# Row maxima from 64-row products in both halves of TensorE's array, with a copy of K on VectorE, a third landing place for weights and a new planned order

## The chip, the cores and the metric

One core of a Trainium2 chip runs the whole program. The time is device microseconds (us) of one execution; three executions of the kernel before took 927.57 to 933.28 us, with a median of 932.64 us. The engines are TensorE (PE, with its weight loads PEld), VectorE (DVE), ScalarE (ACT), GpSimd (POOL) and SyncE (SP), which issues the DMAs.

## The reference

```python
def _attn_ref(q, k, v):                       # (4, 8, 1152, 64) each
    q_pool = q.reshape(B, H, S // 2, 2, D).mean(axis=3)
    scores = np.matmul(q_pool, k.transpose(0, 1, 3, 2)) / np.sqrt(D)
    scores = scores - np.max(scores, axis=-1, keepdims=True)
    attn = np.exp(scores)
    attn = attn / (np.sum(attn, axis=-1, keepdims=True) + 1e-09)
    return np.matmul(attn, v)

def _moe_ref(x, w_in, w_out, a, b):           # x: (2304, 512), w_in: (512, 2048)
    h = x @ w_in
    P = a[0] + a[1] * h + a[2] * h**2 + a[3] * h**3
    Q = 1.0 + np.abs(b[0]) * np.abs(h) + np.abs(b[1]) * h**2
    return (P / (Q + 1e-6)) @ w_out
```

The attention has 4 batches of 8 heads, 576 pooled query rows and 1152 keys per head, depth 64. Its output, 2304 rows of 512, goes through an MLP with a rational function.

## The kernel before, in words

**Numbers in two parts.** Each float32 operand is scaled and split into an upper and a lower float16 part. For a pair of heads (a *unit*), `pr_hi` and `pr_lo` write the parts of K side by side into `spk`, and a DMA transpose (`pr_tr`, L689) turns them: tile `k` then has the 64 depth rows of the upper part of K in partitions 0 to 63 and those of the lower part in 64 to 127. Tile `q` has the upper part of Q twice, in both halves, in its first 9 blocks; its next 9 blocks hold the lower part of Q in partitions 0 to 63 and zeros below. Tile `kb` is a copy of the upper part of K in partitions 0 to 63, made by a DMA (`pr_kb`, L692), and a row of ones at partition 64.

**One attention tile** (144 of them, 128 query rows of one head, or in every ninth, the *wide* slot 8, 64 rows of each of two heads): `at_fill` (L720) makes scores of 128 rows by 1152 keys in the three PSUM banks `SC`, in three products of 384 columns and depth 128 (in a wide tile six, each for 64 output partitions); `at_max` (L727, DVE) takes the negated row maxima; `at_turn` (L730) turns them into a row, and `at_row` (L734, ACT) writes it into `q` at partition 64 beside the lower part. `at_fill2` makes the transposed scores in `ST`, per 128 keys one product of depth 128 (L743) and one of depth 65 (L744), which adds the lower part of Q and the maximum. `at_exp` (L751, ACT) exponentiates into 32-bit whole numbers `E`, `at_split` (L759, DVE) scales their 16-bit halves, and `at_pv` (L773) multiplies by three parts of V, 54 products per group of one or two tiles, into unused columns of the same banks `SC` and `ST`. So a bank is shared in turn by PE, DVE and ACT.

**The MLP** works on 18 chunks of 128 rows in 4 steps each (72): `mo_h` (L915, 48 products), a rational function on ACT, DVE and POOL (L928 to L977), `mo_o` (L986 to L988, 12 products of 512 columns).

**The weights** come in 32 pieces of 512 KB (L458, tile `raw`) into two landing places; ACT and POOL read a piece (L467, L471), DVE joins the bits (L475) into the float32 tile `wf`, ACT squares it for the scale (L480); the split parts follow when all 16 pieces of a matrix are there (L502, L506). The first MLP step can't start before both matrices are done, since its tiles reuse that memory (`w_close`).

**The order** of every engine's work is written out by a planner, `Plan`. Each operation is added with an engine, a duration in ns (a DMA with issue, transfer and lead), a due time and what it reads and writes. The planner simulates forward and backward passes over these durations and keeps the order of the shortest one; `PRM["stir"]` can name seeds of random changes that are tried on it and kept where the planned end comes earlier. Engines then run their instructions strictly in that order. All DMAs are issued by SP in one queue.

Of the kernel before, what the change touches and what calls it, by code (L numbers as in the profile page):

```python
# [23 lines left out]
SLACK = 16.0  # L24
# [6 lines left out]
    stir=[],  # L31
# [238 lines left out]
def kernel(  # L270
# [175 lines left out]
    def w_open():  # L446
        st["stg_cm"] = tc.tile_pool(name="stg", bufs=1)
        st["stg"] = st["stg_cm"].__enter__()

    def w_load(n, i):  # L450

        t = st["stg"].tile([P, 512, 2], I32, tag="raw", name=f"raw_{n}{i}", bufs=NRAW)
        st["raw", n, i] = t
        if n == "wi":
            src = w_in.bitcast(I32)[i // 4 * P:(i // 4 + 1) * P, (i % 4) * 1024:(i % 4 + 1) * 1024]
        else:
            src = w_out.bitcast(I32)[i * P:(i + 1) * P, :]
        nc.sync.dma_start(out=t.rearrange("p f w -> p (f w)"), in_=src)  # L458
# [4 lines left out]
    def w_win(n, i):  # L463
        if i == 0:
            st["wf", n] = st["stg"].tile([P, 16, 512], F32, tag="wf", name=f"wf_{n}")
        u = st["raw", n, i][:, :, 1].bitcast(F32)
        nc.scalar.activation(out=st["wf", n][:, i, :], in_=u, func=AF.Prelu, scale=2.0 ** -111, alpha=-(2.0 ** 32))  # L467
# [203 lines left out]
    def pr_lo(j, w):  # L671
        d = pairs[j]
        stt = nc.vector.scalar_tensor_tensor
        if w == "v":
            stt(pr_new(j, "v2"), d["vn"], d["ss"][:, 2:3], d["v1"][:, :, 0:D], ALU.mult, ALU.subtract)
        elif w == "q":
            stt(spq[:, KC:2 * KC, 0, :], d["qn"][:, :, 0, :], d["ss"][:, 1:2], spq[:, 0:KC, 0, :], ALU.mult, ALU.subtract)
# [13 lines left out]
    def pr_kb(j):  # L691
        nc.sync.dma_start(out=pr_new(j, "kb")[0:D], in_=pairs[j]["k"][0:D])  # L692
# [32 lines left out]

    def at_max(t):
        nc.vector.tensor_reduce(mts[t % NM][:, D:D + 1], SC[:, :, 0:TH], AX.XY, ALU.max, negate=True)  # L727
# [4 lines left out]
    def at_row(t):  # L732
        j, slot = tiles[t]
        nc.scalar.activation(out=pairs[j]["q"][D:D + 1, KC + slot, :], in_=TURN[D:D + 1], func=AF.Copy)  # L734
# [289 lines left out]
    def prep(j, part):  # L1024
# [8 lines left out]
        if mode == "again":  # L1033
            if hp < 2:
                for i in (0, 1) if part == 0 else (2, 3, 4):
                    add("dma", cost(256 * op_cols(i)), at[6], lambda i=i: pr_again(j, i), r=[("kept", bb, hp, i)], w=[("set", o, i)], seq=["seqag"])
                if part == 0:
                    add("dma", (625, 820, 624), at[7], lambda: pr_kb(j), r=[("set", o, 1)], w=[("set", o, 5)])
            return
        if part == 1:  # L1040
            add("act", 1240, at[14], lambda: pr_hi(j, "v"), r=["vn", ("ss", j)], w=[("set", o, 2)])
            add("dve", 1500, at[15], lambda: pr_lo(j, "v"), r=["vn", ("ss", j), ("set", o, 2)], w=[("set", o, 3)])
            add("dve", 370, at[16], lambda: pr_v3(j), r=[("set", o, 2)], w=[("set", o, 4)])
# [5 lines left out]
        add("dma", (1400, 1640, 449), at[0], lambda: pr_load_q(j), w=["qn"])  # L1049
        add("dma", cost(128 * 4608), at[1], lambda: pr_load_v(j), w=["vn"])  # L1050
        add("pool", 1500, at[6], lambda: pr_pool(j), w=["qn"])
        add("act", 1146, at[6], lambda: pr_stat(j, 0), r=["kn"], w=[("st", j), "spk"])
        add("act", 700, at[6], lambda: pr_stat(j, 1), r=["qn"], w=[("st", j), "spk"])
        add("act", 1146, at[6], lambda: pr_stat(j, 2), r=["vn"], w=[("st", j), "spk"])
# [7 lines left out]
        for i, w in enumerate(("k", "q")):  # L1062
            add("act", 1240, at[8 + 2 * i], lambda w=w: pr_hi(j, w), r=[w + "n", ("ss", j)], w=["sp" + w])
            add("dve", 820 if w == "q" else 1650, at[9 + 2 * i], lambda w=w: pr_lo(j, w), r=[w + "n", ("ss", j)], w=["sp" + w])
            add("dma", T_TR2, at[9 + 2 * i], lambda w=w: pr_tr(j, w), r=["sp" + w], w=[("set", o, 0 if w == "q" else 1)])
            if w == "k":
                add("dma", (625, 820, 624), at[10], lambda: pr_kb(j), r=[("set", o, 1)], w=[("set", o, 5)])

    def attend(t):
# [7 lines left out]
        add("pe", (650, 1100) if wide else (490, 960), s, lambda: at_fill(t), r=[("set", o, 0), ("set", o, 1)], w=["S"], seq=["seqS"], bank=B_S)  # L1077
        add("dve", 1330, s + 0.6, lambda: at_max(t), r=["S"], w=[M], bank=B_S)
        add("pe", (60, 128), s + 2.1, lambda: at_turn(t), r=[M], w=["TURN"], seq=["seqM"], bank=B_TURN)
        add("act", 230, s + 2.3, lambda: at_row(t), r=["TURN", ("set", o, 0)], w=[("row", t)], bank=B_TURN)  # L1080
        add("pe", (1150, 2304) if wide else (1010, 2304), s + 2.7, lambda: at_fill2(t), r=[("row", t), ("set", o, 0), ("set", o, 1), ("set", o, 5)], w=["T"], seq=["seqT"], bank=B_T)
        add("act", 1300, s + 3.9, lambda: at_exp(t), r=["T", ("esc", jp)], w=[E], seq=["seqE"], bank=B_T)
        add("dve", 780, s + 5.3, lambda: at_split(t), w=[E], seq=["seql"])

    def product(g, host):
# [6 lines left out]
        add("act", 370, s + PRM["pvx"], lambda: at_x(g), r=[V], w=[x], seq=["seqx"], bank=B_PV[g % 2])  # L1092

    def weights(n, s0):
        for i in range(16):
            s = s0 + PRM["ws"] * i
            raw, wf = ("raw", i % NRAW), ("wf", i)
            add("dma", cost(128 * 4096), s, lambda i=i: w_load(n, i), w=[raw], seq=["raw"])
            add("act", 630, s + 4, lambda i=i: w_win(n, i), r=[raw], w=[wf], seq=["win"])
            add("pool", 830, s + 4, lambda i=i: w_low(n, i), w=[(*raw, "low")], r=[raw], seq=["low"])  # L1100
            add("dve", 800, s + 4, lambda i=i: w_bits(n, i), r=[raw, (*raw, "low")], w=[wf])
            add("act", 615, s + 6, lambda i=i: w_stat(n, i), r=[wf], w=[("wst", n, i)])
# [5 lines left out]
        for i in range(8):  # L1108
            wf = [("wf", 2 * i), ("wf", 2 * i + 1)]
            add("act", 1141, s + PRM["wl"] * i, lambda i=i: w_hi(n, i), r=wf + [("sw", n)], w=[(n, 0, i)])  # L1110
            add("dve", 1330, s + PRM["wl"] * i, lambda i=i: w_lo(n, i), r=wf + [("sw", n), (n, 0, i)], w=[(n, 1, i)])
# [48 lines left out]
    def chunk(p):  # L1160
# [6 lines left out]
        add("dve", 420, u - 1.6, lambda: ch_rcp(c), r=xs + svs, w=["ri"])  # L1167
        add("pool", 1400, u - 1.5, lambda: ch_norm(c), r=["ri"], w=xs)
        add("pool", 870, u, lambda: ch_hi(c), r=xs + [("cf", batches(c)), "late"], w=["xs"])
        add("dve", 900, u, lambda: ch_lo(c), r=xs, w=["xs"])  # L1170
# [4 lines left out]
    def step(p, f):  # L1175
# [92 lines left out]
```

## Time and profile before

| | before |
|---|---|
| median of three executions | 932.64 us (927.57 to 933.28) |
| profiled execution | 926.45 us, span of its instructions 924.7 us |
| granted TensorE clock, mean | 0.954 |
| PE busy | 809.6 us, 88% |
| DVE busy | 750.5 us, 81% |
| ACT busy | 620.5 us, 67% |
| POOL busy | 445.4 us, 48% |
| bytes moved by DMA | 88.80 MB |

Busy is the time in which at least one instruction of an engine runs. Matmuls overlap: one of 128 columns is listed with about 220 ns, and the next starts 56 ns after it, so the distance from start to start tells what a product costs PE in a stream. PEclk is the granted clock as a share of 2.4 GHz. An "idle" figure of a row is the engine's idle time just before that instruction, with the instruction or transfer that ended it.

### The profile page before, as it was taken

How to read it: one execution, taken by the hardware profiler on the slowest of the kernel's cores; microseconds unless marked ns; L12 is line 12 of the kernel's file. 1: busy time of each engine (PE TensorE's matmuls, PEld its weight loads, DVE VectorE, ACT ScalarE, POOL GpSimd, SP SyncE). 2: the span in 40 equal slices, each digit the busy share in tenths (PEclk: the TensorE clock that was granted, in tenths of full speed). 3: DMA queues.
4: the chain of work that ended last, by engine and by line, in shares of the span. 5: the costliest groups of instructions: out<-in, count | busy, mean ns of one | idle time of the engine just before them, and what ended most of it. 6: DMA issues, size and time to landing. Idle time of an engine off the chain costs nothing.

```text
span 924.7 us, 27851 instructions
## 1 busy us (share of the span) xinstructions
PE 809.6 (88%) x12196; PEld 640.1 (69%) x12196; DVE 750.5 (81%) x1011; ACT 620.5 (67%) x937; POOL 445.4 (48%) x482
## 2 busy tenths in 40 slices
PE   0687587649999999899899999989999998999997
PEld 0475366537878887677678886777777777887773
DVE  5578887787988988769899888779989867977666
ACT  5579988765767767646856786666767746665452
POOL 3212235315755624458655552446855454445664
PEclk9988778958999999979999999989999999999999
DMA  7587376801600706612501234290917300521000
GB/s 217 160 210 199 80 189 214 222 24 44 135 25 1 155 2 154 144 34 48 119 13 26 44 112 91 73 245 14 236 32 155 70 20 14 164 68 25 24 13 23
DMA packets 121338, 88.80 MB, mean 96 GB/s; under 512 B 96768, under 2 KB 98816, under 8 KB 121216
## 3 DMA queue, kind: packets, MB, share of 16 engines
q1 hardware_dynamic: 121216, 87.02, 38.2%
q8 instruction: 95, 1.56, 0.7%
q14 instruction: 27, 0.22, 0.1%
HBM read 49.24 MB, written 8.87 MB: 63 GB/s over the span
## 4 chain that ended last, share of the span: by engine, by line
PE 54%; DVE 17%; ACT 11%; DMA 6%; issue 5%; POOL 4%; SPq 2%; POOLq 0%; DVEq 0%; ACTq 0%
PE ph_h L915 14%; PE st L743 6%; PE st L744 6%; PE sc L773 6%; PE st L773 5%; PE sc L720 5%; PE po L986 4%; PE po L988 4%; PE po L987 4%; ACT E L751 4%; DVE mt L727 3%; DVE E L759 2%; DVE t L941 2%; DVE g L965 2%; DVE t L937 2%
## 5 line engine op out<-in xcount | busy, mean ns | idle before, releaser
L751 ACT ACTIVATE E<-st,esc 128x1152 int32<-128x1152 f32 x144 | 188.6, 1310 | 68.3 <-PE st L730 45.7
L727 DVE TENSOR_REDUCE mt<-sc 128x1 f16<-128x1152 f32 x144 | 194.8, 1353 | 43.9 <-PE sc L720 32.5
L915 PEld LDWEIGHTS <-wi 128*128 128x128 f16 x3456 | 199.6, 99 | 24.2 <-DVE t L941 15.8
L915 PE MATMUL ph_h<-x,wi 128*128 128x128 f16 x3312 | 201.6, 221 | 10.5 <-DVE t L941 8.6
L743 PE MATMUL st<-q,k 128*128 128x128 f16 (+1 forms) x1440 | 179.4, 222 | 17.6 <-ACT q L734 12.2
L744 PE MATMUL st<-q,kb 65*128 65x128 f16 (+1 forms) x1440 | 179.8, 222 | 2.5 <-DMA kb<-k 2.5
L973 POOL TENSOR_TENSOR e<-t,e 128x512 f32<-128x512 f32 x72 | 111.4, 1547 | 141.3 <-DVE e L969 118.7
L744 PEld LDWEIGHTS <-kb 65*128 65x128 f16 x1440 | 137.8, 102 | 27.2 <-issue 21.0
L773 PEld LDWEIGHTS <-E 128*128 128x128 f16 (+1 forms) x4320 | 146.9, 103 | 11.5 <-issue 7.1
L743 PEld LDWEIGHTS <-k 128*128 128x128 f16 x1440 | 137.7, 102 | 17.2 <-issue 12.3
L759 DVE TENSOR_SCALAR E<-E 128x2304 f16<-128x2304 uint16 x144 | 126.8, 883 | 27.4 <-ACT E L751 27.2
L720 PE MATMUL sc<-k,q 128*128 128x384 f16 (+1 forms) x480 | 104.2, 353 | 41.2 <-DVE mt L727 28.6
L946 POOL TENSOR_SCALAR e<-A,b_abs 128x512 f32<-128x512 f32 x72 | 71.2, 989 | 82.5 <-ACT A L928 82.0
L988 PE MATMUL po<-wo,g 128*128 128x512 f16 x288 | 109.1, 379 | 1.6 <-DVE g L977 1.6
L986 PE MATMUL po<-wo,g 128*128 128x512 f16 x288 | 109.2, 379 | 0.0
L987 PE MATMUL po<-wo,g 128*128 128x512 f16 x288 | 109.1, 379 | 0.0
L950 POOL TENSOR_TENSOR e<-e,A 128x512 f32<-128x512 f32 x72 | 97.1, 1348 | 5.5
L720 PEld LDWEIGHTS <-q 128*128 128x128 f16 (+1 forms) x480 | 40.4, 105 | 73.7 <-issue 44.4
L928 ACT ACTIVATE A<-ph_h,cf 128x512 f32<-128x512 f32 x69 | 47.3, 685 | 58.5 <-PE ph_h L915 56.0
L954 ACT ACTIVATE A<-e,q_one 128x512 f32<-128x512 f32 x72 | 51.9, 720 | 48.3 <-POOL e L950 47.6
L977 DVE SCALAR_TENSOR_TENSOR g<-e,cf,A 128x512 f16<-128x512 f32 x72 | 64.9, 901 | 21.4 <-POOL e L973 21.3
L773 PE MATMUL sc<-v,E 128*128 128x65 f16 (+3 forms) x2160 | 77.3, 198 | 0.0
(124 smaller groups left out, 1175.7 us busy)
## 6 DMA issues: line engine op xcount, KB each, us to landing
kn<-in_k_dram SPq DMA_DIRECT2D x16, 576.0 KB, 4.5
vn<-in_v_dram SPq DMA_DIRECT2D x16, 576.0 KB, 5.2
qn<-in_q_dram SPq DMA_DIRECT2D x16, 512.0 KB, 4.9
raw_wi<-in_moe_w_in_dram SPq DMA_DIRECT2D x16, 512.0 KB, 4.8
raw_wo<-in_moe_w_out_dram SPq DMA_DIRECT2D x16, 512.0 KB, 4.5
kb<-k SPq DMA_DIRECT2D x18, 288.0 KB, 5.0
out_dram<-ob SPq DMA_DIRECT2D x16, 256.0 KB, 3.4
keep<-v SPq DMA_DIRECT2D x4, 292.5 KB, 5.7
```

The lines of the kernel that those rows point to most:

```text
L720: nc.tensor.matmul(SC[ps, jj, 0:TH], d["q"][:, slot, ps], d["k"][:, h * KC + 3 * jj:h * KC + 3 * jj + 3, :].rearrange("p c m -> p (c m)"), ...
L727: nc.vector.tensor_reduce(mts[t % NM][:, D:D + 1], SC[:, :, 0:TH], AX.XY, ALU.max, negate=True)
L743: nc.tensor.matmul(o, d["k"][:, h * KC + c, :], d["q"][:, slot, qs], start=True, stop=False)
L744: nc.tensor.matmul(o, d["kb"][0:D + 1, h * KC + c, :], d["q"][0:D + 1, KC + slot, qs], start=False, stop=True)
L751: nc.scalar.activation(out=d["e"].rearrange("p (a c) -> p a c", a=3), in_=ST[:, :, 0:TH], func=AF.Exp, bias=esc[:, 1:2], scale=esc[:, 0:1],)
L759: nc.vector.tensor_scalar(e.bitcast(F16), e.bitcast(U16), 2.0 ** -6, None, ALU.mult)
L773: nc.tensor.matmul(pv[:, 0:w], e[:, c, qs, part], pairs[j][n_v][:, h * KC + c, :], start=(c == 0 and i == 0), stop=(c == KC - 1 and i == 2),)
L915: nc.tensor.matmul(mo[c, f]["p2"][:, i, :], wi[wl][:, kk, fs], x[:, xl * KD + kk, :], start=(n == 0), stop=(n == 3 * KD - 1))
L973: nc.gpsimd.tensor_tensor(w["e2"], w["t"], w["e2"], ALU.subtract)
L986: nc.tensor.matmul(po, g[0][:, e, :], wo[0][:, kk, :], start=(kk == 0), stop=False)
L987: nc.tensor.matmul(po, g[0][:, e, :], wo[1][:, kk, :], start=False, stop=False)
L988: nc.tensor.matmul(po, g[1][:, e, :], wo[0][:, kk, :], start=False, stop=(kk == KF - 1))
```

## The change

The row maxima are taken from the upper parts of Q and K alone: `at_fill` makes products of depth 64 in place of 128, the first and third of a tile with partitions 0 to 63 (`k`), the second with partitions 64 to 127, where a copy of the upper part of K now lies in `kb`. The exponent's bias has more room for that (`SLACK` 24 in place of 16). The lower part of Q therefore moves to partitions 64 to 127, the row of maxima to partition 0, and the second product of `at_fill2` has depth 128 in place of 65. The copy of K is made by DVE in place of a DMA. Weight pieces 2, 5, 8 and 11 of each matrix land in the last sixteenths of `wf` in place of `raw`. In the planner's table most durations are new, loads are counted at 270 in place of 360 bytes per ns, and 25 seeds are tried.

```diff
-SLACK = 16.0
+SLACK = 24.0
...
-    stir=[],
+    stir=[5001, 5004, 5032, 5039, 5073, 5194, 5227, 5228, 5235, 5238, 5243, 5266, 5295, 5296, 5303, 5333, 5337, 5459, 5480, 5488, 5573, 5643, 5745, 5890, 5998],
...
-    T_COPY, T_TR2 = 450, (625, 3050, 625)
+    T_COPY, T_TR2 = 450, (625, 3300, 625)
     def cost(n_bytes):
-        return (T_COPY, n_bytes / 360.0, T_COPY - 1)
+        return (T_COPY, n_bytes / 270.0, T_COPY - 1)
...
         for t in kbs:
-            nc.vector.memset(t[D:D + 1], 1.0)
-        nc.gpsimd.memset(spq[:, KC:2 * KC, 1, :], 0.0)
+            nc.vector.memset(t[0:D], 0.0)
+            nc.vector.memset(t[0:1], 1.0)
+        nc.gpsimd.memset(spq[:, KC:2 * KC, 0, :], 0.0)
...
+        st["wf", "wi"] = st["wf", "wo"] = st["stg"].tile([P, 16, 512], F32, tag="wf", name="wf")
+    IN_WF = (2, 5, 8, 11)
     def w_load(n, i):
-        t = st["stg"].tile([P, 512, 2], I32, tag="raw", name=f"raw_{n}{i}", bufs=NRAW)
+        if i in IN_WF:
+            t = st["wf", n][:, 14:16, :].bitcast(I32).rearrange("p a (f w) -> p (a f) w", w=2)
+        else:
+            t = st["stg"].tile([P, 512, 2], I32, tag="raw", name=f"raw_{n}{i}", bufs=NRAW)
...
     def pr_kb(j):
-        nc.sync.dma_start(out=pr_new(j, "kb")[0:D], in_=pairs[j]["k"][0:D])
+        nc.vector.tensor_copy(pr_new(j, "kb")[D:P], pairs[j]["k"][0:D])
...
         for jj in range(3):
+            half = slice(D, P) if jj == 1 else slice(0, D)
...
-                    SC[ps, jj, 0:TH], d["q"][:, slot, ps],
-                    d["k"][:, h * KC + 3 * jj:h * KC + 3 * jj + 3, :].rearrange("p c m -> p (c m)"),
+                    SC[ps, jj, 0:TH], d["q"][half, slot, ps],
+                    d[("k", "kb", "k")[jj]][half, h * KC + 3 * jj:h * KC + 3 * jj + 3, :].rearrange("p c m -> p (c m)"),
...
-                nc.tensor.matmul(o, d["kb"][0:D + 1, h * KC + c, :], d["q"][0:D + 1, KC + slot, qs], start=False, stop=True)
+                nc.tensor.matmul(o, d["kb"][:, h * KC + c, :], d["q"][:, KC + slot, qs], start=False, stop=True)
...
-                add("dma", (625, 820, 624), at[10], lambda: pr_kb(j), r=[("set", o, 1)], w=[("set", o, 5)])
+                add("dve", 710, at[10], lambda: pr_kb(j), w=[("set", o, 1)])
...
-        add("dve", 780, s + 5.3, lambda: at_split(t), w=[E], seq=["seql"])
+        add("dve", 870, s + 5.3, lambda: at_split(t), w=[E], seq=["seql"])
...
-        add("dve", 800, u + PRM["m_glo"], lambda: mo_glo(c, f), r=[A], w=[G, E2, T])
+        add("dve", 900, u + PRM["m_glo"], lambda: mo_glo(c, f), r=[A], w=[G, E2, T])
```

The copy writes the resource ("set", o, 1), which `at_fill` reads, so a unit's first scores wait for its copy.

## Rows read from the trace of the kernel before

**Rows 1.** The page's span in 40 slices of 23.1 us: busy tenths of PE.
```profile
PE   0687587649999999899899999989999998999997
```

**Rows 2.** Busy time of the engines in four stretches: up to the first MLP step, then two with attention and MLP steps together and, between them, one almost without MLP steps. Columns: stretch, its length, busy us of PE, PEld, DVE, ACT, POOL with the count of instructions, granted clock, DMA share, GB/s.
```profile
25.00:211.00 186.00, 123.74 (x1754) 97.06 (x1752) 144.93 (x202) 145.93 (x236) 52.39 (x72) 0.83 0.61 161
211.00:331.00 120.00, 116.76 (x1906) 97.99 (x1905) 104.62 (x129) 85.44 (x121) 72.06 (x60) 0.98 0.32 67
331.00:402.00 71.00, 67.22 (x1007) 50.16 (x1004) 54.78 (x87) 46.00 (x69) 25.70 (x50) 0.93 0.46 104
402.00:546.00 144.00, 138.67 (x2147) 112.89 (x2146) 128.83 (x159) 99.38 (x146) 87.78 (x75) 1.00 0.26 60
```

**Rows 3.** The chain of waits up to 215 us, some of its longest pieces. Columns: start, length, what.
```profile
24.99 7.89 DMA kb<-k
...
148.47 3.38 DMA raw_wo<-in_moe_w_out_dram
...
171.45 4.54 DMA raw_wo<-in_moe_w_out_dram
...
178.09 3.05 DMA raw_wo<-in_moe_w_out_dram
...
196.57 9.65 DVE wo L506 x8
...
211.42 3.59 PE ph_h L915 x33
```

**Rows 4.** What the DMA queue on SP waited for before it issued loads of weight pieces (us in total, times, longest), and the issues of the second matrix (ns min/median/max, first and last start).
```profile
SPq L458 <- DVE wf_wi L475: 16.9, 7, 9.8
...
SPq L458 <- DVE wf_wo L475: 11.4, 7, 2.3
...
L458 SPq DMA_DIRECT2D raw_wo<-in_moe_w_out_dram x16: 327/335/715, 125.9 to 180.8; - x16
```

**Rows 5.** PE in order of time around the three score products of an ordinary tile. Columns: start, length of the piece, instruction, shapes, count.
```profile
363.55 0.38 PE L988 MATMUL po<-wo,g 128*128 128x512 f16 x1
363.76 0.65 PE L720 MATMUL sc<-k,q 128*128 128x384 f16 x3
364.25 0.22 PE L743 MATMUL st<-q,k 128*128 128x128 f16 x1
```

**Rows 6.** The same around the six score products of a wide tile, each of which fills 64 columns of the array, in pairs.
```profile
708.88 0.38 PE L988 MATMUL po<-wo,g 128*128 128x512 f16 x1
709.19 0.68 PE L720 MATMUL sc<-k,q 128*64 128x384 f16 x6
709.80 0.39 PE L986 MATMUL po<-wo,g 128*128 128x512 f16 x1
```

**Rows 7.** The same where a product of depth 3 and 4 columns stands between products of depth 128.
```profile
345.27 0.65 PE L720 MATMUL sc<-k,q 128*128 128x384 f16 x3
345.85 0.17 PE L358 MATMUL sc<-diag,onesb 3*128 3x4 bf16 x1
345.96 0.23 PE L743 MATMUL st<-q,k 128*128 128x128 f16 x1
```

**Rows 8.** Groups of instructions by form: the score products of ordinary and of wide tiles. Columns: line, engine, operation, tiles, shapes, count, busy us and mean ns, idle before with its releasers.
```profile
L720 PE MATMUL sc<-k,q 128*128 128x384 f16 x384 | 92.6, 354 | 39.5 <-DVE mt L727 27.2 <-DMA q<-spq 11.3 <-DVE top L350 0.9
...
L720 PE MATMUL sc<-k,q 128*64 128x384 f16 x96 | 11.5, 350 | 1.7 <-DVE mt L727 1.5 <-ACT xf L790 0.2
```

**Rows 9.** Waits after 210 us: how long the maxima stood for the score products (us in total, times, longest).
```profile
DVE mt L727 <- PE sc L720: 20.2, 29, 2.6
```

**Rows 10.** Single lines: the split of E (2304 columns of 16 bits) and the third part of V (1170 such columns) on DVE, the issue of the copy of K, each with ns min/median/max and first and last start; and from issue to landing, first of the 32 transposes, then of the 18 copies of K.
```profile
L759 DVE TENSOR_SCALAR E<-E x144: 728/753/1836, 37.9 to 841.7; 128x2304 f16<-128x2304 uint16 x144
...
L684 DVE TENSOR_SCALAR v<-v x16: 450/460/1701, 20.3 to 751.0; 128x1170 f16<-128x1170 f16 x16
...
L692 SPq DMA_DIRECT2D kb<-k x18: 476/532/701, 25.0 to 811.0; - x18
...
DMA to landing us min/median/max: 4.6/6.1/8.3
...
DMA to landing us min/median/max: 3.2/5.0/9.8
```

**Rows 11.** PE and SP near the start, in order of time.
```profile
23.88 1.14 PE L720 MATMUL sc<-k,q 128*128 128x384 f16 x3 [11.33 <-DMA q<-spq]
...
30.09 0.31 PE L743 MATMUL st<-q,k 128*128 128x128 f16 x1
...
32.92 0.29 PE L744 MATMUL st<-q,kb 65*128 65x128 f16 x1 [2.52 <-DMA kb<-k]
```

**Rows 12.** Groups of DVE instructions: five whose planned durations the change raises, and the memsets of `kb`. Columns as in rows 8.
```profile
L727 DVE TENSOR_REDUCE mt<-sc 128x1 f16<-128x1152 f32 x144 | 194.8, 1353 | 43.9 <-PE sc L720 32.5 <-PE sc L358 5.9 <-PE sc L773 1.9
L759 DVE TENSOR_SCALAR E<-E 128x2304 f16<-128x2304 uint16 x144 | 126.8, 883 | 27.4 <-ACT E L751 27.2
...
L977 DVE SCALAR_TENSOR_TENSOR g<-e,cf,A 128x512 f16<-128x512 f32 x72 | 64.9, 901 | 21.4 <-POOL e L973 21.3
L965 DVE SCALAR_TENSOR_TENSOR g<-t,cf,A 128x512 f16<-128x512 f32 x72 | 59.3, 824 | 10.8 <-ACT A L958 9.7 <-PE po L987 0.8
...
L684 DVE TENSOR_SCALAR v<-v 128x1170 f16<-128x1170 f16 x16 | 11.3, 704 | 0.0
...
L434 DVE MEMSET kb<- 1x2304 f16 x2 | 4.0, 1978 | 0.9 <-issue 0.9
```

More of the change, by code (lines that the diff above doesn't have):

```diff
@@ L463, in w_win @@
     def w_win(n, i):
-        if i == 0:
-            st["wf", n] = st["stg"].tile([P, 16, 512], F32, tag="wf", name=f"wf_{n}")
         u = st["raw", n, i][:, :, 1].bitcast(F32)
@@ L676, in pr_lo @@
         elif w == "q":
-            stt(spq[:, KC:2 * KC, 0, :], d["qn"][:, :, 0, :], d["ss"][:, 1:2], spq[:, 0:KC, 0, :], ALU.mult, ALU.subtract)
+            stt(spq[:, KC:2 * KC, 1, :], d["qn"][:, :, 0, :], d["ss"][:, 1:2], spq[:, 0:KC, 0, :], ALU.mult, ALU.subtract)
         else:
@@ L726, in at_max @@
     def at_max(t):
-        nc.vector.tensor_reduce(mts[t % NM][:, D:D + 1], SC[:, :, 0:TH], AX.XY, ALU.max, negate=True)
+        nc.vector.tensor_reduce(mts[t % NM][:, 0:1], SC[:, :, 0:TH], AX.XY, ALU.max, negate=True)
     def at_turn(t):
@@ L733, in at_row @@
         j, slot = tiles[t]
-        nc.scalar.activation(out=pairs[j]["q"][D:D + 1, KC + slot, :], in_=TURN[D:D + 1], func=AF.Copy)
+        nc.scalar.activation(out=pairs[j]["q"][0:1, KC + slot, :], in_=TURN[0:1], func=AF.Copy)
     def at_fill2(t):
@@ L1037, in prep @@
                 if part == 0:
-                    add("dma", (625, 820, 624), at[7], lambda: pr_kb(j), r=[("set", o, 1)], w=[("set", o, 5)])
+                    add("dve", 710, at[7], lambda: pr_kb(j), w=[("set", o, 1)])
             return
@@ L1041, in prep @@
             add("act", 1240, at[14], lambda: pr_hi(j, "v"), r=["vn", ("ss", j)], w=[("set", o, 2)])
-            add("dve", 1500, at[15], lambda: pr_lo(j, "v"), r=["vn", ("ss", j), ("set", o, 2)], w=[("set", o, 3)])
-            add("dve", 370, at[16], lambda: pr_v3(j), r=[("set", o, 2)], w=[("set", o, 4)])
+            add("dve", 1600, at[15], lambda: pr_lo(j, "v"), r=["vn", ("ss", j), ("set", o, 2)], w=[("set", o, 3)])
+            add("dve", 705, at[16], lambda: pr_v3(j), r=[("set", o, 2)], w=[("set", o, 4)])
             if mode == "first" and hp < 2:
@@ L1048, in prep @@
         add("dma", cost(128 * 4608), at[0], lambda: pr_load_k(j), w=["kn"])
-        add("dma", (1400, 1640, 449), at[0], lambda: pr_load_q(j), w=["qn"])
+        add("dma", (1400, 2200, 449), at[0], lambda: pr_load_q(j), w=["qn"])
         add("dma", cost(128 * 4608), at[1], lambda: pr_load_v(j), w=["vn"])
         add("pool", 1500, at[6], lambda: pr_pool(j), w=["qn"])
-        add("act", 1146, at[6], lambda: pr_stat(j, 0), r=["kn"], w=[("st", j), "spk"])
-        add("act", 700, at[6], lambda: pr_stat(j, 1), r=["qn"], w=[("st", j), "spk"])
-        add("act", 1146, at[6], lambda: pr_stat(j, 2), r=["vn"], w=[("st", j), "spk"])
+        add("act", 1255, at[6], lambda: pr_stat(j, 0), r=["kn"], w=[("st", j), "spk"])
+        add("act", 773, at[6], lambda: pr_stat(j, 1), r=["qn"], w=[("st", j), "spk"])
+        add("act", 1255, at[6], lambda: pr_stat(j, 2), r=["vn"], w=[("st", j), "spk"])
         chain(at[7], half_exp(lambda: pairs[j]["st"]), w=[("st", j)])
@@ L1063, in prep @@
             add("act", 1240, at[8 + 2 * i], lambda w=w: pr_hi(j, w), r=[w + "n", ("ss", j)], w=["sp" + w])
-            add("dve", 820 if w == "q" else 1650, at[9 + 2 * i], lambda w=w: pr_lo(j, w), r=[w + "n", ("ss", j)], w=["sp" + w])
+            add("dve", 850 if w == "q" else 1560, at[9 + 2 * i], lambda w=w: pr_lo(j, w), r=[w + "n", ("ss", j)], w=["sp" + w])
             add("dma", T_TR2, at[9 + 2 * i], lambda w=w: pr_tr(j, w), r=["sp" + w], w=[("set", o, 0 if w == "q" else 1)])
             if w == "k":
-                add("dma", (625, 820, 624), at[10], lambda: pr_kb(j), r=[("set", o, 1)], w=[("set", o, 5)])
+                add("dve", 710, at[10], lambda: pr_kb(j), w=[("set", o, 1)])
     def attend(t):
@@ L1076, in attend @@
         wide = slot == 8
-        add("pe", (650, 1100) if wide else (490, 960), s, lambda: at_fill(t), r=[("set", o, 0), ("set", o, 1)], w=["S"], seq=["seqS"], bank=B_S)
-        add("dve", 1330, s + 0.6, lambda: at_max(t), r=["S"], w=[M], bank=B_S)
+        add("pe", (600, 1100) if wide else (390, 960), s, lambda: at_fill(t), r=[("set", o, 0), ("set", o, 1)], w=["S"], seq=["seqS"], bank=B_S)
+        add("dve", 1353, s + 0.6, lambda: at_max(t), r=["S"], w=[M], bank=B_S)
         add("pe", (60, 128), s + 2.1, lambda: at_turn(t), r=[M], w=["TURN"], seq=["seqM"], bank=B_TURN)
-        add("act", 230, s + 2.3, lambda: at_row(t), r=["TURN", ("set", o, 0)], w=[("row", t)], bank=B_TURN)
-        add("pe", (1150, 2304) if wide else (1010, 2304), s + 2.7, lambda: at_fill2(t), r=[("row", t), ("set", o, 0), ("set", o, 1), ("set", o, 5)], w=["T"], seq=["seqT"], bank=B_T)
+        add("act", 268, s + 2.3, lambda: at_row(t), r=["TURN", ("set", o, 0)], w=[("row", t)], bank=B_TURN)
+        add("pe", (1150, 2304) if wide else (1010, 2304), s + 2.7, lambda: at_fill2(t), r=[("row", t), ("set", o, 0), ("set", o, 1)], w=["T"], seq=["seqT"], bank=B_T)
         add("act", 1300, s + 3.9, lambda: at_exp(t), r=["T", ("esc", jp)], w=[E], seq=["seqE"], bank=B_T)
-        add("dve", 780, s + 5.3, lambda: at_split(t), w=[E], seq=["seql"])
+        add("dve", 870, s + 5.3, lambda: at_split(t), w=[E], seq=["seql"])
     def product(g, host):
@@ L1091, in product @@
         add("pe", (1600, 3000), s, lambda: at_pv(g), r=[("set", j % 2, i) for i in (2, 3, 4)] + [("E", t % NE) for t in groups[g]], w=[V], seq=["seqP"], bank=B_PV[g % 2])
-        add("act", 370, s + PRM["pvx"], lambda: at_x(g), r=[V], w=[x], seq=["seqx"], bank=B_PV[g % 2])
+        add("act", 276, s + PRM["pvx"], lambda: at_x(g), r=[V], w=[x], seq=["seqx"], bank=B_PV[g % 2])
     def weights(n, s0):
@@ L1096, in weights @@
             s = s0 + PRM["ws"] * i
-            raw, wf = ("raw", i % NRAW), ("wf", i)
+            home = sum(j not in IN_WF for j in range(i)) % NRAW
+            raw, wf = ("wf", 14) if i in IN_WF else ("raw", home), ("wf", min(i, 14))
             add("dma", cost(128 * 4096), s, lambda i=i: w_load(n, i), w=[raw], seq=["raw"])
[L1099 to L1102, printed above, removed]
+            add("act", 670, s + 4, lambda i=i: w_win(n, i), r=[raw], w=[wf], seq=["win"])
+            add("pool", 830, s + 4, lambda i=i: w_low(n, i), w=[("low", n, i)], r=[raw], seq=["low"])
+            add("dve", 715, s + 4, lambda i=i: w_bits(n, i), r=[raw, ("low", n, i)] if raw != wf else [("low", n, i)], w=[wf])
+            add("act", 715, s + 6, lambda i=i: w_stat(n, i), r=[wf], w=[("wst", n, i)])
         s = s0 + 16 * PRM["ws"] + 2
@@ L1108, in weights @@
         for i in range(8):
-            wf = [("wf", 2 * i), ("wf", 2 * i + 1)]
+            wf = [("wf", min(2 * i, 14)), ("wf", min(2 * i + 1, 14))]
             add("act", 1141, s + PRM["wl"] * i, lambda i=i: w_hi(n, i), r=wf + [("sw", n)], w=[(n, 0, i)])
-            add("dve", 1330, s + PRM["wl"] * i, lambda i=i: w_lo(n, i), r=wf + [("sw", n), (n, 0, i)], w=[(n, 1, i)])
+            add("dve", 1280, s + PRM["wl"] * i, lambda i=i: w_lo(n, i), r=wf + [("sw", n), (n, 0, i)], w=[(n, 1, i)])
         s += 8 * PRM["wl"]
@@ L1166, in chunk @@
         svs = [("sv", bb, hp, 0) if c < 4 * B else ("sv", b_, hp, 1) for hp in range(NPAIR) for b_ in batches(c)]
[L1167 to L1170, printed above, removed]
+        add("dve", 515, u - 1.6, lambda: ch_rcp(c), r=xs + svs, w=["ri"])
+        add("pool", 1250, u - 1.5, lambda: ch_norm(c), r=["ri"], w=xs)
+        add("pool", 950, u, lambda: ch_hi(c), r=xs + [("cf", batches(c)), "late"], w=["xs"])
+        add("dve", 850, u, lambda: ch_lo(c), r=xs, w=["xs"])
         add("dma", (625, 900, 625), u, lambda: ch_tr(c), r=["xs"], w=[("X", p % XB)])
@@ L1194, in step @@
         add("act", 620, u + PRM["m_ln"], lambda: mo_r(c, f), w=[A])
-        add("dve", 750, u + PRM["m_ghi"], lambda: mo_ghi(c, f), r=[T, A], w=[G], seq=["seqG"])
-        add("dve", 770, u + PRM["m_d1"], lambda: mo_d1(c, f), r=[G], w=[E2])
-        add("pool", 1400, u + PRM["m_rem"], lambda: mo_rem(c, f), r=[T], w=[E2])
-        add("dve", 800, u + PRM["m_glo"], lambda: mo_glo(c, f), r=[A], w=[G, E2, T])
+        add("dve", 820, u + PRM["m_ghi"], lambda: mo_ghi(c, f), r=[T, A], w=[G], seq=["seqG"])
+        add("dve", 805, u + PRM["m_d1"], lambda: mo_d1(c, f), r=[G], w=[E2])
+        add("pool", 1530, u + PRM["m_rem"], lambda: mo_rem(c, f), r=[T], w=[E2])
+        add("dve", 900, u + PRM["m_glo"], lambda: mo_glo(c, f), r=[A], w=[G, E2, T])
         po = "po_t" if last else "po"
```

## The prediction, made before the change was run

> **What bounds the kernel now.** I read the slices first, then the busy time by stage, then the chain of waits, then single instructions in order of time. The slices show two regimes: in the first nine PE is busy 4 to 8 tenths, afterwards 8 to 9 or more [rows 1]. The table by stage gives sizes. From 25 to 211 us PE is busy 123.74 of 186 us, DVE 144.93 and ACT 145.93, so no engine is full and latencies decide; the granted clock has a mean of 0.83, a mix of 1.2 and 2.4 GHz. After 211 us PE is busy 116.76 of 120, 67.22 of 71 and 138.67 of 144 us, DVE up to 128.83 of 144 [rows 2]. So a nanosecond of PE counts after 211 us, and DVE is the next limit, at 89% in the busiest stretch. In the first stage the chain runs through a copy of K (7.89 us), late weight pieces and, at its end, 9.65 us of DVE on the second matrix, right before the first MLP step at 211.42 us [rows 3].
>
> **The change part by part.** The sum is against the profiled execution, 926.45 us; the median of the runs is 932.64, 0.7% above, and I carry the sum over to that median.
>
> *First copy of K.* The first second-pass product stands at 30.09 us until the copy lands; the next starts at 32.92, after 2.52 us of idle PE [rows 11]. With a copy on DVE this wait goes: K's transpose lands before Q's, and Q's releases the first scores at 23.88, so a copy of under 1 us fits before it. What is late next is the ACT chain of the first tiles. I take -2.5 us; bounds 0 (ACT absorbs it) and -7.9 (the whole piece of the chain). The memsets of `kb` grow by 64 rows of as many columns each, about 4 us more at the 1.98 us of a row [rows 12]; they run while DVE waits for the first loads, and would cost those 4 us without that cover.
>
> *Third landing place.* SP stood 16.9 and 11.4 us until DVE had emptied a landing place [rows 4], and the chain holds three waits for pieces of the second matrix, 3.38, 4.54 and 3.05 us, together 10.97 [rows 3]. Sixteen loads were issued in 54.9 us, one per 3.4 us [rows 4]; with three places in turn up to piece 11, a load may go out about one such interval earlier, which is the size of each wait. Only pieces 12 to 15 keep two places. Behind the weights ACT and DVE are 78% busy, so part of the time comes back as waits on them. I take -8; bounds 0 and -16 (the three waits and a similar share in the first matrix). Loads counted slower (270 bytes per ns) only make the planner issue them earlier; in the term for the order.
>
> *Score products.* An ordinary tile's three products hold PE from 363.76 to 364.25, 0.49 us [rows 5], 0.16 each. In the new form the first two lie in different halves of the array. Nothing of depth 64 is in the trace, but the wide tiles have pairs side by side in the other direction: six products end 0.68 us after their start, three full ones 0.65 [rows 5, 6]. So pairs do run together, and two of the three products should take the time of one: 0.33 us. Against that stands the passage between shapes of the array. The wide fill starts 0.31 us after a product of 512 columns that otherwise gives way after 0.21, and what follows starts 0.61 us after the fill's start where three pairs need 0.49 [rows 5, 6]: 0.09 in and 0.12 out. A product of depth 3 shows it in the direction of this change: it starts 0.58 us after the fill in front of it, not 0.49, and although it has 4 columns the next start is 0.11 later [rows 7]. So the new ordinary fill costs 0.09 + 0.33 + 0.12 = 0.54 us, 0.05 more than now, 6.4 us over 128 tiles; a wide fill falls from 0.70 to the same 0.54, 2.6 us less over 16 (384 and 96 products [rows 8]). That is +3.8 on PE, +2.7 for the seven tenths of the tiles that lie after 211 us. The last product starts 0.07 us earlier than now, which the maxima feel where they wait for it, 29 times after 210 us [rows 9], 2.0 us. Net +1. Bounds: passages cost nothing, 0.16 x 128 + 0.37 x 16 = -26; halves don't overlap, 0.70 for 0.49, +27.
>
> The Trainium skill, in TensorEngine Tiling (Array Packing), section Key Properties, says that changing the tiling mode drains TensorE. The trace agrees: the 0.09 to 0.12 us above. By the up to two-fold speed that its section Theoretical Speedup gives for depths up to 64, with no drain, the term would be about -20 us.
>
> The second product of `at_fill2` has depth 128 for 65; both shapes already follow each other at one interval of 0.06 us, so nothing. ACT's row and DVE's maxima change partition alone, nothing.
>
> *Copy of K on DVE.* Eighteen copies of 2304 columns of 16 bits. The nearest row is the split of E, as many columns of the same width: median 0.753, mean 0.883, longest 1.836 us; below it 0.450 for 1170 columns [rows 10, 12]. So 13.6 to 15.9 us of DVE, bounds 8 and 33. SP loses 18 issues of 0.53 us. New is a wait: DVE runs in order, so it stands at the copy until K's transpose has landed, 4.6 to 8.3 us after issue, median 6.1 [rows 10]; the planner's own figures make this about 5.5, so an ordinary copy may stand 0.6 us, a late one 2.8. Behind it stand a tile's maximum or a split, and PE waits for those. Six copies fall into the first stage, where DVE has 41 us free; of the twelve others, 0.88 + 0.6 us each, 17.8 together, I put a bit over a quarter on the path: +5. Bounds 0 and +50 (18 x 2.8).
>
> *New order.* The old durations were short for DVE: 23 ns x 144 for the maxima, 103 x 144 for the split, 101 x 72 and 74 x 72 in the MLP, 334 x 16 for V, 36 us in all [rows 12], 5% of DVE's work, so the old order ran late against its own plan just where DVE is fullest. The new figures are near the measured means. What an order can win back after 211 us is PE's idle time, 3.2 + 3.8 + 5.3 us in three stretches of together 335 us [rows 2], so at that rate an estimated 26 us over the 714 us to the end. I take nearly a third, -8. It can also lose: the seeds are kept by the planner's end, not the chip's. Bounds -26 and +15 (the same share lost twice over).
>
> Sum: -2.5 - 8 + 1 + 5 - 8 = -12.5 us, 914 for an execution like the profiled one, 920 on the median.
>
> **Rivals.** *No real change:* weights come earlier but ACT and DVE take up the wait, and the new order is no better: -2.5 + 1 + 5 = +3.5, about 936. For it speaks that both engines are at 78% in the first stage [rows 2].
>
> *Passages between shapes hide* (PE is often idle before a fill, 39.5 us of idle time stand before ordinary score products [rows 8]): -26 in place of +1, of which seven tenths count, -18, so 901. Against it: the passages seen in the trace stand in dense streams [rows 6, 7].
>
> *DVE held by K's landing (slower).* If each copy stands 2.8 us and takes 0.88, DVE is blocked 18 x 3.7 = 66 us; with half of it on the path the term is +33, and the other parts give -17.5: about +20 on the median with the waits that follow, 948. It decides from a mean wait of some 2 us. For it: landings vary by 3.7 us [rows 10]; against it: the planner knows the dependence and can leave room.
>
> *Halves one after the other* (the parts side by side don't do what they should): +27, seven tenths of it +19, in place of +1: about 938. Against it: the pairs of the wide tiles [rows 6].
>
> **Numbers.** Forecast 0.40 (908 to 930), no real change 0.28, hidden passages 0.15, DVE held 0.10, halves in sequence 0.07. The likeliest gives 920. About one per cent, 923 to 942 on the median, is what measurement can tell from no change. Faster by more: nearly all of the forecast's lower two thirds and above that the hidden passages, with a little of the second case, 0.51. Slower by more: DVE held, half of the sequence case and the tail of the second, 0.17. Within: 0.32. The range reaches from the hidden passages' 901 to past the sequence case, 900 to 944.
>
> **What would show it.** In the changed profile: first scores near 24 us and no stop at the first second-pass products; first MLP step near 200 us in place of 211; an ordinary fill with its second product a few ns after the first, its next neighbour about 0.45 us after the start when dense and 0.09 before it; copies on DVE of 0.75 to 0.9 us with idle time before them named after K's transposes, under 1 us each; PE's idle time after 211 us below 26 us. The forecast is wrong if the first MLP step does not move, if fills take 0.33 or 0.70, or if DVE's idle time before copies passes 30 us.

## The result and the profile after

The changed kernel takes 887.44 us (886.09 to 891.47, four executions) against 932.52 us: a ratio of 0.953, 95% interval 0.949 to 0.958. The forecast of 920 us and its range of 900 to 944 are missed: the direction was right, the size far too small. The profiled execution took 888.17 us, its span 886.4 us, at a mean granted clock of 0.971 (0.954 before). DVE's busy share rose from 81 to 87%.

The busy times by stretch of the changed kernel, cut as in [rows 2] at the first MLP step and around the pause in MLP steps (302 to 310 us is left out), with the same columns:

```profile
25.00:182.00 157.00, 108.77 (x1667) 84.07 (x1668) 137.81 (x193) 133.01 (x224) 47.15 (x69) 0.86 0.65 178
182.00:302.00 120.00, 117.99 (x1962) 96.14 (x1961) 111.63 (x143) 85.03 (x131) 65.54 (x59) 0.99 0.29 62
310.00:370.00 60.00, 55.71 (x884) 39.06 (x880) 50.46 (x68) 38.22 (x61) 23.81 (x39) 0.98 0.53 113
370.00:514.00 144.00, 141.38 (x2240) 112.01 (x2240) 135.35 (x177) 97.75 (x150) 95.16 (x87) 0.99 0.24 56
```

The first stage is 157 us long, not 186, and DVE fills 88% of it, not 78%. In the busiest stretch DVE has reached 94% [rows 2]. The chain of waits near the first MLP step, which stood at 211.42 us [rows 3]:

```profile
124.72 3.81 DMA raw_wo<-in_moe_w_out_dram
...
165.67 7.17 DVE wo L512 x6
...
181.73 2.45 PE ph_h L922 x24
```

One long wait for a piece of the second matrix is left of three, and the first MLP step begins 29.7 us earlier, by when 31 tiles have reached the exponential, against 32 before. So of the 38.3 us that the span lost, 29.7 lie ahead of that step and 8.6 behind it. The queue's waits for a landing place did not shrink, however (28.3 us in [rows 4]); the loads simply go out earlier, as the line's own view shows in the second fence:

```profile
SPq L466 <- DVE wf L481: 33.7, 15, 4.1
```

```profile
L466 SPq DMA_DIRECT2D raw_wo<-in_moe_w_out_dram x12: 327/328/535, 99.6 to 146.4; - x12
```

An ordinary fill in a dense stream, as in [rows 5], and a wide one, as in [rows 6], PE in order of time:

```profile
265.68 0.38 PE L995 MATMUL po<-wo,g 128*128 128x512 f16 x1
266.00 0.33 PE L727 MATMUL sc<-k,q 64*128 64x384 f16 x1
266.00 0.33 PE L727 MATMUL sc<-kb,q 64*128 64x384 f16 x1
266.17 0.32 PE L727 MATMUL sc<-k,q 64*128 64x384 f16 x1
266.42 0.39 PE L993 MATMUL po<-wo,g 128*128 128x512 f16 x1
...
480.28 0.38 PE L995 MATMUL po<-wo,g 128*128 128x512 f16 x1
480.59 0.35 PE L727 MATMUL sc<-k,q 64*64 64x384 f16 x2
480.60 0.35 PE L727 MATMUL sc<-kb,q 64*64 64x384 f16 x2
480.78 0.33 PE L727 MATMUL sc<-k,q 64*64 64x384 f16 x2
481.03 0.23 PE L737 MATMUL st<-ident,mt 128*128 128x128 f16 x1
```

The halves run together: the second product starts with the first, the third 0.17 us later. But the fill starts 0.32 us after a product that gives way after 0.215, and what follows it starts 0.25 us after the last product: 0.105 + 0.17 + 0.25, about 0.53 us where 0.49 stood. The wide one takes 0.095 + 0.44, 0.54 us, where it took 0.70.

The line of the copy of K (ns min/median/max), and the first tiles in order of time:

```profile
L698 DVE COPY kb<-k x18: 753/754/1719, 21.7 to 772.0; 64x2304 f16<-64x2304 f16 x18
```

```profile
26.23 0.50 PE L727 MATMUL sc<-k,q 64*128 64x384 f16 x1 [13.89 <-DMA q<-spq]
...
29.87 0.27 PE L750 MATMUL st<-q,k 128*128 128x128 f16 x1 [0.35 <-ACT q L741]
29.93 0.31 PE L751 MATMUL st<-q,kb 128*128 128x128 f16 x1
...
32.10 1.29 ACT L758 ACTIVATE E<-st,esc 128x1152 int32<-128x1152 f32 x1
```

The second pass no longer stops after one product [rows 11]; the first exponential starts at 32.10 us, where it started at 34.95, although the first scores come 2.35 us later.

### The profile page after: what moved, and what is told of

Same layout as the page of the kernel before. It is cut to its first block, busy times and chain, and to the rows that moved or that the text cites. A ratio compares the mean times of both kernels' runs of the same rounds, so it can differ in the third digit from the quotient of the medians.

```text
span 886.4 us, 27822 instructions
## 1 busy us (share of the span) xinstructions
PE 785.8 (89%) x12196; PEld 605.4 (68%) x12196; DVE 775.1 (87%) x1031; ACT 594.5 (67%) x937; POOL 449.1 (51%) x482
## 4 chain that ended last, share of the span: by engine, by line
PE 59%; DVE 22%; ACT 8%; issue 4%; DMA 4%; POOL 2%; SPq 1%; DVEq 0%; ACTq 0%; POOLq 0%
PE ph_h L922 16%; PE sc L780 6%; PE st L750 6%; PE st L751 6%; PE po L993 5%; DVE mt L734 5%; PE po L995 5%; PE st L780 5%; PE po L994 5%; PE sc L727 4%; DVE E L766 3%; ACT E L758 2%; DVE g L984 2%; DVE t L944 2%; DVE t L948 2%
## 5 line engine op out<-in xcount | busy, mean ns | idle before, releaser
L750 PE MATMUL st<-q,k 128*128 128x128 f16 (+1 forms) x1440 | 171.8, 221 | 11.6 <-ACT q L741 6.5
L751 PE MATMUL st<-q,kb 128*128 128x128 f16 (+1 forms) x1440 | 171.8, 221 | 0.0
L980 POOL TENSOR_TENSOR e<-t,e 128x512 f32<-128x512 f32 x72 | 107.2, 1489 | 96.3 <-DVE e L976 91.8
L780 PEld LDWEIGHTS <-E 128*128 128x128 f16 (+1 forms) x4320 | 143.0, 102 | 18.0 <-issue 11.5
L751 PEld LDWEIGHTS <-kb 128*128 128x128 f16 x1440 | 135.9, 101 | 15.1 <-issue 11.6
L953 POOL TENSOR_SCALAR e<-A,b_abs 128x512 f32<-128x512 f32 x72 | 80.3, 1115 | 125.9 <-ACT A L935 125.8
L766 DVE TENSOR_SCALAR E<-E 128x2304 f16<-128x2304 uint16 x144 | 124.5, 874 | 8.0 <-ACT E L758 7.7
L727 PE MATMUL sc<-k,q 64*128 64x384 f16 (+1 forms) x320 | 76.7, 349 | 33.8 <-DVE mt L734 19.0
L984 DVE SCALAR_TENSOR_TENSOR g<-e,cf,A 128x512 f16<-128x512 f32 x72 | 71.3, 992 | 6.6 <-POOL e L980 6.5
L780 PE MATMUL st<-v,E 128*128 128x65 f16 (+3 forms) x2160 | 72.9, 194 | 3.5 <-ACT E L758 2.3
```

Of the source, the lines that this page charges most:

```text
L727: nc.tensor.matmul(SC[ps, jj, 0:TH], d["q"][half, slot, ps], d[("k", "kb", "k")[jj]][half, h * KC + 3 * jj:h * KC + 3 * jj + 3, :].rearran ...
L751: nc.tensor.matmul(o, d["kb"][:, h * KC + c, :], d["q"][:, KC + slot, qs], start=False, stop=True)
L766: nc.vector.tensor_scalar(e.bitcast(F16), e.bitcast(U16), 2.0 ** -6, None, ALU.mult)
L780: nc.tensor.matmul(pv[:, 0:w], e[:, c, qs, part], pairs[j][n_v][:, h * KC + c, :], start=(c == 0 and i == 0), stop=(c == KC - 1 and i == 2),)
L980: nc.gpsimd.tensor_tensor(w["e2"], w["t"], w["e2"], ALU.subtract)
```

## The experiments

All times are medians; ratios are to the kernel before on the same chip, whose medians lay between 928.7 and 932.5 us. The changed kernel's parts are called products, copy (of K on DVE), place (the third one), table (of durations) and seeds.

**One part undone, the order kept.** These two show what a part costs with every other instruction at its place.

```diff
-            half = slice(D, P) if jj == 1 else slice(0, D)
...
-                    SC[ps, jj, 0:TH], d["q"][half, slot, ps],
-                    d[("k", "kb", "k")[jj]][half, h * KC ...
+                    SC[ps, jj, 0:TH], d["q"][:, slot, ps],
+                    d["k"][:, h * KC ...
```

> The changed kernel with its score products at the old depth of 128 from k alone, every instruction in the same order. Theory 1 (the gain lies in the order and the landing place, not in the products): an ordinary fill falls from 0.53 to 0.49 us of PE, a wide one rises from 0.54 to 0.70, so 885 to 891 us, within 0.5% of the changed kernel. Theory 2 (the maxima start earlier and this shortens the chain through the bank of scores): 897 us or more.

885.46 us, 0.952 (0.947 to 0.956). An ordinary fill is back at 0.49 us:

```profile
265.11 0.65 PE L726 MATMUL sc<-k,q 128*128 128x384 f16 x3
265.60 0.38 PE L992 MATMUL po<-wo,g 128*128 128x512 f16 x1
```

It can't be told from the changed kernel: the products that name the change give nothing that shows. Theory 2 falls. The two differ in the mean granted clock as well, 0.979 to 0.983 in the four executions here against 0.967 to 0.971, so what the products cost at one and the same clock is not shown.

```diff
-        nc.vector.tensor_copy(pr_new(j, "kb")[D:P], pairs[j]["k"][0:D])
+        nc.sync.dma_start(out=pr_new(j, "kb")[D:P], in_=pairs[j]["k"][0:D])
```

> The changed kernel with the copy of K by DMA again, issued at the same place of the order. DVE loses 18 copies of 0.75 us, 13.6 us in all, but the first scores of a unit now need the copy, which lands some 5 us after its issue. Theory 1: between -4 and +6 us, 883 to 894, since the order leaves room before most units. Theory 2 (the copy on DVE is a main part of the gain, because units start sooner): 900 us or more.

892.71 us, 0.960 (0.954 to 0.965): 5 us above the changed kernel, with overlapping intervals. The waits that the copy's landing now causes are few:

```profile
PE sc L727 <- DMA kb<-k: 4.1, 3, 2.5
```

**The seeds and the place taken out.** From here on the planner makes a new order.

```diff
-    stir=[5001, ..., 5998],
+    stir=[],
```

> The changed kernel planned without the 25 seeds. Theory 1: the random tries are worth 8 to 20 us, so 895 to 907. Theory 2: under 5 us, 887 to 892.

912.70 us, 0.980 (0.974 to 0.986): the seeds are worth 25 us, more than theory 1 gave them. The intervals don't overlap. Busy time before and after the first MLP step, first without seeds, then the changed kernel behind its step (its first stage is shown above):

```profile
25.00:197.00 172.00, 116.35 (x1737) 91.34 (x1737) 142.54 (x204) 137.66 (x230) 52.55 (x73) 0.81 0.61 162
197.00:913.00 716.00, 679.95 (x10454) 524.43 (x10454) 615.22 (x794) 443.34 (x680) 379.42 (x393) 0.98 0.29 69
```

```profile
182.00:886.00 704.00, 676.61 (x10530) 521.15 (x10528) 620.31 (x805) 446.29 (x686) 392.11 (x395) 0.99 0.30 71
```

The same work in another order: DVE's share of the first stage goes from 83 to 88%, the first step from 197 to 182 us, and the rest from 716 to 704 us.

```diff
-    IN_WF = (2, 5, 8, 11)
+    IN_WF = ()
```

> The changed kernel with two landing places for weight pieces, planned anew with the same table and seeds. Theory 1: the weights are done later, the first MLP step moves from 182 us back to 190 to 200, and the time rises by 8 to 15 us, 895 to 902. Theory 2: under 5 us, 887 to 892.

909.52 us, 0.979 (0.973 to 0.985), above both theories. That looks like 22 us for the place, but the seeds were found for another plan. So both edits were made together:

> The changed kernel with two landing places and without seeds. The 25 seeds were given for the plan with three places; on another plan they are 25 random tries. Theory 1a (the third place is worth time by itself): 8 us or more above the plan with three places and no seeds, 920 to 935. Theory 1b (the third place matters only because the seeds fit its plan): within 5 us of that plan, 908 to 918.

919.20 us, 0.988 (0.985 to 0.992): 6.5 us above three places without seeds, between theories 1a and 1b. Next, all old durations put back, no seeds, three places (two lines of the edit):

```diff
-        add("dve", 870, s + 5.3, lambda: at_split(t), w=[E], seq=["seql"])
+        add("dve", 780, s + 5.3, lambda: at_split(t), w=[E], seq=["seql"])
...
-    stir=[5001, ..., 5998],
+    stir=[],
```

> The changed kernel with the old durations in the planner's table (the copy of K keeps its 710 ns) and without seeds: products, copy on DVE and third place alone. Theory 1c (durations near the measured means are worth time): 5 us or more above the new table without seeds, 918 to 932. Rival (the table only deals the cards anew): within 5 us of it on either side, 908 to 918.

910.70 us, 0.980 (0.974 to 0.985), as with the new table: without seeds the table is worth nothing on this plan. Theory 1c fails here.

**Parts added to the kernel before.**

```diff
+    IN_WF = (2, 5, 8, 11)
...
+        if i in IN_WF:
+            t = st["wf", n][:, 14:16, :].bitcast(I32).rearrange("p a (f w) -> p (a f) w", w=2)
...
```

> The kernel before with the third landing place as the only change, old table, no seeds. Theory 1a: 918 to 925, 8 us or more below the kernel before, first MLP step before 205 us. Theory 1b: within 5 us of the kernel before, 926 to 936.

927.55 us, 0.998 (0.995 to 1.001): no change that can be told. Yet the first MLP step moves as theory 1a has it:

```profile
202.34 2.72 PE ph_h L919 x24
```

Nine us earlier than before; in a span of 925.7 us the rest then takes 723 us, where it took 713. An earlier first step is not yet a gain. With the new durations on top, and those of the old products kept:

```diff
+        add("dve", 870, s + 5.3, lambda: at_split(t), w=[E], seq=["seql"])
-        add("dve", 780, s + 5.3, lambda: at_split(t), w=[E], seq=["seql"])
...
```

> The kernel before with the third landing place and the new durations (those of the old products kept), no seeds; products and copy of K as before. Against the changed kernel without seeds it lacks only the products and the copy on DVE. If these two are worth nothing by themselves, 907 to 918; if the copy on DVE is worth several us in the plan, 920 to 930.

919.06 us, 0.989 (0.981 to 0.996), between the two expectations. Place and table together give about 1%; products and copy bring this to the 0.980 of the run without seeds, with intervals that overlap.

**The same search for every plan.** The seeds 5000 to 5999 are tried in turn on each plan and kept where its planned end comes earlier; on the changed plan this gives just the change's 25. "Other" seeds are from 6000 to 6999, the third draw from 7000 to 7999. Only `stir` and the part named differ; for the kernel before the whole edit is

```diff
-    stir=[],
+    stir=[5004, 5025, 5043, 5063, 5066, 5071, 5080, 5089, 5091, 5100, 5168, 5176, 5573, 5593, 5622, 5833, 5931],
```

> The changed kernel with two landing places, with 21 seeds found for its own plan in the way the change's 25 were found (the seeds 5000 to 5999 in turn, kept where the planned end comes earlier). Theory 1 (the search pays wherever the table is true; the third place by itself is worth some 6 us, as without seeds): 890 to 900. Rival (the third place is what the good orders use): 905 or more, no better than with the foreign seeds.

912.61 us, 0.981 (0.975 to 0.987): the rival's range.

> The changed kernel with the old table of durations, with 16 seeds found for its own plan among the same 1000. Theory 1 (a search on a plan that runs late on the chip finds orders that the chip doesn't follow): 5 us or less below the old table without seeds, 904 to 912. Rival (any search pays as much): 20 us or more below it, 885 to 893.

903.38 us, 0.973 (0.967 to 0.979): 7 us below the old table without seeds, just outside theory 1's range and far from the rival's.

> The kernel before with third place, new table and 15 seeds found for its own plan among the same 1000; products of depth 128 and the copy of K by DMA. What it lacks against the changed kernel are the products and the copy on DVE, at an equal search. If they are worth only the 5 us of the copy in a fixed order: 890 to 897. If the copy on DVE matters for what orders there are: 900 or more.

901.62 us, 0.970 (0.965 to 0.976): the second expectation.

> The kernel before with nothing but 17 seeds found for its own plan among the same 1000, old table. Theory 1: under 8 us below the kernel before, 923 to 931, since the table is not true. Rival (any search pays as much): 20 us or more, 905 to 912.

916.63 us, 0.986 (0.979 to 0.993): a search alone gives the kernel before some 13 us, although its table is short. Theory 1's reason, that a search pays only on a true table, falls; so does the rival's 20 us.

> The changed kernel with 20 seeds found for its plan among 6000 to 6999 in place of the 25 found among 5000 to 5999. If the search is worth about the same whatever the seeds: 887 to 898, 15 us or more below the plan without seeds. If the change's 25 were a lucky draw: 899 or more.

902.31 us, 0.969 (0.967 to 0.972). The same kernel with another draw of the same size is 15 us slower than with its own. Its stages:

```profile
25.00:191.00 166.00, 113.93 (x1700) 88.28 (x1698) 146.08 (x200) 136.18 (x232) 49.31 (x70) 0.87 0.65 169
191.00:901.00 710.00, 680.74 (x10493) 525.93 (x10492) 608.59 (x798) 443.52 (x678) 396.90 (x395) 0.98 0.30 70
```

Both stages lie between those without seeds and those of the change. The mean granted clock, 0.948 to 0.957, is like that without seeds (0.951 to 0.959).

> The changed kernel with two landing places and 20 seeds found for its own plan among 6000 to 6999. If two places really cost some 20 us at an equal search: 905 to 915 as with the first draw. If the first draw was a poor one: 890 to 900.

903.12 us, 0.969 (0.965 to 0.972): the first draw for two places was a poor one.

> The kernel before with third place and new table, products and copy of K as before, 29 seeds found for its own plan among 6000 to 6999. If products and copy on DVE are worth only what the fixed orders show, -2 and 5 us: 886 to 895. If they are worth 10 us or more at an equal search: 898 to 906 as with the first draw.

898.24 us, 0.964 (0.962 to 0.967): the edge of the second expectation, but the two draws of this plan and the three of the changed one overlap.

> The changed kernel with 12 seeds found for its plan among 7000 to 7999, a third draw. If the draws scatter by some 15 us and the change's is the best of them: 892 to 905. If 902 was the exception: 885 to 890.

896.69 us, 0.964 (0.960 to 0.968): the change's draw is the best of three. This one is laid out otherwise:

```profile
25.00:194.00 169.00, 118.55 (x1744) 92.93 (x1745) 139.57 (x199) 134.81 (x228) 50.17 (x69) 0.82 0.60 166
194.00:895.00 701.00, 672.14 (x10452) 516.33 (x10450) 614.63 (x798) 443.80 (x681) 397.54 (x395) 0.99 0.31 71
```

Its first stage is hardly shorter than without seeds, the rest shorter than the change's.

> The changed kernel with score products of depth 128, planned anew with the old durations for them and 18 seeds found for that plan among 5000 to 5999; third place, table and the copy on DVE stay. If the form of the products is worth nothing, a draw like the others: 890 to 905. If it matters for what orders there are: 908 or more.

892.27 us, 0.959 (0.955 to 0.963): products of full depth, with an order of their own, lie between the draws of the depth-64 plan.

Ratios, plan by plan:

| plan | no seeds | draws |
|---|---|---|
| before | 1 | 0.986 |
| before, place and table | 0.989 | 0.970, 0.964 |
| changed, two places | 0.988 | 0.981, 0.969 |
| changed, old table | 0.980 | 0.973 |
| changed, full depth | | 0.959 |
| changed | 0.980 | **0.953**, 0.969, 0.964 |

**The version that the prices point to**, depth 64 in wide tiles alone, in the order of the change:

```diff
-            half = slice(D, P) if jj == 1 else slice(0, D)
+            half = slice(0, P) if slot < 8 else slice(D, P) if jj == 1 else slice(0, D)
...
```

> The changed kernel in its own order, with products of depth 64 in the wide tiles alone (0.54 us for 0.70) and of depth 128 in the ordinary ones (0.50 for 0.53). By these prices 128 x 0.03 = 3.8 us less on PE: 883 to 887, just below the changed kernel and below the run with full depth everywhere or level with it. If the earlier start of the maxima counts: 888 or more.

886.01 us, 0.952 (0.949 to 0.955): below both kernels by its median, but not to be told from the changed one, as with full depth everywhere.

## Why the prediction was wrong, point by point

**The order is the step that failed.** Its term was -8 us, "nearly a third" of PE's idle time after the first MLP step, with a lower bound of -26. Seeds alone measured -25 (no_seeds against the change). The term looked at one stage and one engine: of the 26.8 us between those two spans, 15.6 came ahead of the first step, where the forecast gave the order nothing and put everything on the landing place, and 11 behind it. The reason given is not borne out either: durations nearer to the measured means did not make the order better without seeds (old_table_no_seeds), and a search pays on the old table too (before_own_seeds). One entry of the new table even went the other way: it counts an ordinary fill at 390 ns in place of 490, and the trace shows 0.53 us. About 9 to 15 us of the gain is this draw: the other two on the same plan end at 896.7 and 902.3 us. That a draw can be worth more than any part was not in the sum.

The seeds are not the whole miss. Without them the changed plan stands 19 us below the kernel before (912.70 against 931.38), where the terms other than the order sum to -4.5. The old table gives the same 0.980, so the durations don't account for these 14 us; which part or which new deal they come from stays open.

By what path an order pays is not shown. The mean granted clock went with the time: 0.967 to 0.971 in the four executions of the change, 0.951 to 0.959 without seeds. In one kernel too: the seven executions of the kernel before beside no_seeds run from 923.27 us at 0.963 to 933.65 us at 0.946. So part of an order's gain may come by the clock, and no run separates it. It need not be all: other_seeds, at a clock like that without seeds, is still 10 us faster.

**Third landing place, -8.** The first half of the mechanism was right: the place brings the first step 9 us forward, from 211.4 to 202.3 us in the kernel before and from 206.6 to 197.3 in the changed one without seeds. That this comes off the end isn't borne out: two_places_other_seeds has its first step at 202.4 us and ends with other_seeds, which has it at 191.3. As for size, it gave 3 us alone, not to be told from nothing, and 0.8% of ratio without seeds; with seeds the mean of two draws with two places is 0.975, that of three with three places 0.962, and the draws of the two plans overlap. What it is worth between 0 and some 12 us stays open.

**Score products, +1.** Right in mechanism and in the price of a fill. Forecast 0.54 us for both fills, measured 0.53 and 0.54 in dense streams; undone in the same order, the time doesn't change by more than can be told. The drain between tiling modes, which the Trainium skill states in TensorEngine Tiling (Array Packing), section Key Properties, fits the 0.105 and 0.09 us on either side of the products in half of the array. The rivals of hidden passages (-18) and of halves in sequence (+19) fall: undone, the time should have risen by 18 us or dropped by 19, and it is 2 us lower.

**Copy of K on DVE, +5.** Its median duration is the forecast's lower price, 0.754 us, but longer ones bring the 18 to the upper price, 15.9 us. The wait behind K's transpose did not come, so that rival falls too; DVE's idle time before all 18 copies is 0.7 us:

```profile
L698 DVE COPY kb<-k 64x2304 f16<-64x2304 f16 x18 | 15.9, 886 | 0.7
```

Put back on the DMA queue in the same order the copy costs about 5 us more, so the term probably has the wrong sign; the intervals overlap, and it is not shown. (The parts that the prediction lists for the rival of DVE held by K's landing sum to +15.5; its 948 us stands on that, not on "about +20".)

**Start, -2.5.** The first exponential starts 2.85 us earlier, as forecast, although the first scores come at 26.23 us and not near 24. The memsets of 64 rows take 2.0 us together, where 4 more were forecast. What of this reaches the end no run separates.

**Idle time and the next limit.** PE's idle time behind the first step, said to fall below 26 us, is about 27 (704.00 - 676.61). DVE's share in the busiest stretch rose from 89 to 94%.

Not settled: what place, table and the pair of products and copy are worth one by one. Added to the kernel before in that order they give ratios of 0.998, 0.989 and 0.980; each step deals a new order, and orders of one plan scatter by 0.6 to 1.6%.

## What to carry to other kernels

Where a planner writes out the order, a change to its input is first of all a new deal: measure a part with the order kept, and compare plans over several draws before a part gets the credit. A search over orders is a change of its own: its three draws on the changed plan gave 10 to 25 us, where all other parts together gave some 19. Where it pays differs by draw, so the idle time of one engine in one stage is no measure of it: against no seeds the change's draw gained 15.6 us ahead of the first MLP step, the third draw 4 us there and 15 behind it. A product of half depth in half of the array pays only if what running side by side saves is more than the two passages, 0.2 us here: three products of 384 columns came out 0.04 us dearer, six of a wide tile 0.16 us cheaper, and neither shows in the time of the whole.

## What the runs showed of the hardware

Four products run side by side in quarters of the array: in a wide fill the first four start within 10 ns, and the whole takes 0.54 us, hardly longer than an ordinary one (0.53). The passage into and out of halves costs about the same as into and out of columns (0.105 and 0.09 us against 0.09 and 0.12). A DVE copy from partitions 0 to 63 into 64 to 127 takes as long (0.754 us) as the split of as many columns in all 128 partitions in place (0.753 [rows 10]), by the medians. In one kernel, before, the mean granted clock ran from 0.946 to 0.963 from execution to execution, with 933.65 and 923.27 us.
